# Gate and value products of a SwiGLU block: three float32r passes of split operands in place of seven float32 products

## The chip, the core and the metric

The kernel runs on one core of a Trainium2 chip. The metric is device microseconds (us) of one execution. Five engines work beside each other, each through its own instructions in order: PE (TensorE, the matrix products), DVE (VectorE), ACT (ScalarE), POOL (GpSimd) and SP (SyncE, which issues DMA transfers here). The products accumulate in PSUM, which has eight banks of 128 x 512 float32; all else lies in SBUF.

## The reference

A Mamba-2 scan over 4 batches, 8 heads and 768 positions (head dimension 32, state 16) feeds a SwiGLU block with RMS norm over 3072 tokens, width 256 and hidden width 1536. The weights come in float64.

```python
for c in range(nc):                       # chunks of 32
    CB = einsum('bhin,bhjn->bhij', Cc, Bc)
    y_intra = einsum('bhij,bhjd->bhid', CB * L, xc)       # L: causal decays
    y_inter = einsum('bhin,bhnd->bhid', Cc, state) * decay_to_i
    state = decay_full * state + sum_j(Bx * decay_from_j)
x = y.transpose(0, 2, 1, 3).reshape(3072, 256)
xn = x / sqrt(mean(x * x) + 1e-6) * rms_g
g = xn @ w_gate                           # 3072 x 256 @ 256 x 1536
val = xn @ w_val
return (g * sigmoid(g) * val) @ w_out     # 3072 x 1536 @ 1536 x 256
```

## The kernel before

The tokens go in six blocks of 512. While the gate, value and output products of one block run, the scan of the next block runs between them (transposes `turn`, products `g` and `y`, decays `L`), then its norm (`sq`, `ms`, `rs`, `rb`, `xn`). The normed block `xns[blk]` holds two halves of the width (128 partitions each) by 512 tokens.

**Order.** A string `order` lists about 1550 steps `block:name.numbers`; each step issues a few instructions, and so every engine's queue follows that string. Nothing is moved afterwards. SP's queue gets the transfers in the same order: weights (`fetch`, L160), inputs (`bc`, L121; `x`, L128), decays of later blocks (`spread`, L461), outputs.

**Weights.** Twenty pieces of float64 weights are fetched as pairs of 32-bit words and made into float32 by ACT (`pow`, L182 to L185: the power of two) and DVE (`man`, L192 and L195: the mantissa; `wt`, L201: their product, written to `wgv` or `wo`). All of it lies in block 0.

**Gate and value products.** Block 0 computes columns 0 to 767 (f = 0 to 5, 128 columns each) by plain float32 products (L827, and L837 before the norm is known). Everything else, three pairs of f in block 0 and six pairs in each of blocks 1 to 5, uses Winograd's form of a 2 x 2 block product: seven products instead of eight (`P`, L911) for a pair of f, gate and value side by side in a bank. Each is two float32 matmuls of 128 x 256, and the compiler makes two instructions of one float32 matmul. The form needs sums of weights (`cw`, L881, four DVE instructions for each j), sums of the normed block (`tx`, L888), copies of the running sum out of PSUM (`take`, L917, ACT) and additions (`C`, L923, DVE); then SiLU (`silu`, L932, ACT) and its product with the value (`hid`, L936, DVE). Two banks are tagged gate, two val.

**Output products.** Block 0 uses plain products (`o`, L943); blocks 1 to 5 use the same seven-product form (`O`, L1001) with sums `two` of `w_out` and sums `s`, `s2`, `s3`, `s4` of the hidden tile.

Of the kernel before, what the change touches and what calls it, by code (L numbers as in the profile page):

```python
# [9 lines left out]
FP32 = mybir.dt.float32  # L10
I32 = mybir.dt.int32
I16 = mybir.dt.int16
U32 = mybir.dt.uint32
BF16 = mybir.dt.bfloat16
# [6 lines left out]
def kernel(  # L21
# [108 lines left out]

    wgv = const.tile([P, 2, 2, DF], FP32, name="wgv")
    wg, wv = wgv[:, 0], wgv[:, 1]
# [10 lines left out]
    wdst = {"g": wg, "v": wv, "o": wo}  # L143
# [5 lines left out]
    def fetch(*ks):  # L149
        for k in ks:  # L150
            n, c, w = pieces[k]
            if n == "o":
                src, dst, shape = wsrc[n][:, c:c + w], wo[:, c:c + w], (w, DM)
            else:
                src, dst = wsrc[n][:, :, 2 * c:2 * (c + w)], wdst[n][:, :, c:c + w]
                shape = (2, w)
# [41 lines left out]
    def weight(k):  # L198
        words16, (lo, hi), dst, shape = fetched[k]
        e, f = parts.pop((k, "e")), parts.pop((k, "f"))  # L200
        nc.vector.scalar_tensor_tensor(out=dst, in0=f, scalar=2.0 ** -20, in1=e,  # L201
                                       op0=ALU.mult, op1=ALU.mult)

    a_sb = ffn.tile([BH, S], FP32, tag="ob", name="a_sb", bufs=1)
    warm = const.tile([P, 256], BF16, name="warm")
    gcol = const.tile([P, 2], FP32, name="gcol")
    ident = const.tile([P, P], FP32, name="ident")
    ones = const.tile([P, P], FP32, name="ones")
    upto = const.tile([P, P], FP32, name="upto")
    never = const.tile([P, P], FP32, name="never")  # L210
    after = const.tile([P, P], FP32, name="after")
    chunk_ones = const.tile([P, 2, P], FP32, name="chunk_ones")
# [7 lines left out]
    ident16 = const.tile([P, P], BF16, name="ident16")  # L220
    never16 = const.tile([P, HC], BF16, name="never16")
    whole16 = const.tile([P, P], BF16, name="whole16")
# [11 lines left out]
    la4 = [const.tile([P, 4, 4, NH], FP32, name="la4%d" % k) for k in range(2)]  # L234
# [124 lines left out]
    def three_parts(k):  # L359
        r_ps = ps.pop(("r", k))  # L360
        first = nrm.tile([P, 2, P], BF16, tag="first", name="first", bufs=1)
# [4 lines left out]
        second = nrm.tile([P, 2, P], BF16, tag="second", name="second", bufs=1)  # L366
        nc.vector.tensor_copy(out=second, in_=rest)
        rows[k] = row = const.tile([P, 2, P], BF16, name="row%d" % k)
# [44 lines left out]
    def pair_tile(g):  # L413
        p = g // 2
        if p not in Ls and p < 4:
            Ls[p] = ssd.tile([P, 2, NH, P if p < 2 else HC], FP32, tag="L", name="L", bufs=2)
        elif p not in Ls:
            Ls["of", p // 2] = L = ssd.tile([P, 4, NH, HC], FP32, tag="L", name="L", bufs=2)
            for k in range(2):
                Ls[p - p % 2 + k] = L[:, 2 * k:2 * k + 2]  # L420
# [213 lines left out]
    def states(p):  # L634
        A_ps = ps.pop(("A", p))
        b, c0, chunks = chunks_of(p)
        new = ssd.tile([P, 2, 2, 2, D], FP32, tag="A", name="A")
# [161 lines left out]
    def norm_apply(blk):  # L799
        r = ps["r", blk]  # L800
        xns[blk] = nrm.tile([P, 2, TB], FP32, tag="xn", name="xn", bufs=1)
        if blk:
            for t in range(2):
# [3 lines left out]
        else:  # L807
            nc.vector.tensor_tensor(out=xns[0], in0=yts[0],
                                    in1=r.unsqueeze(1).to_broadcast([P, 2, TB]), op=ALU.mult)

# [29 lines left out]

    def of_block_0(f):
        return hidden_tile(0, f // 2)[:, f % 2].rearrange("p k m -> p (k m)")

    def normed(f):
        gv = ps.pop(("gv", f))
        us[f] = ffn.tile([P, TB], FP32, tag="u", name="u", bufs=2)
# [3 lines left out]
    def silu_of(f):  # L850
        if f not in us:
            us[f] = ffn.tile([P, TB], FP32, tag="u", name="u", bufs=2)
# [16 lines left out]
    Sw, Tx = {}, {}  # L869

    def combine_w(j):
        if j < NF // 4:
            s = raw.tile([P, 2, 4, P], FP32, tag="wr", name="sw", bufs=6)
        else:
            s = const.tile([P, 2, 4, P], FP32, name="sw%d" % j)
        Sw[j] = s
        f1, f2 = slice(2 * j * P, (2 * j + 1) * P), slice((2 * j + 1) * P, (2 * j + 2) * P)
        a11, a12, a21, a22 = wgv[:, :, 0, f1], wgv[:, :, 1, f1], wgv[:, :, 0, f2], wgv[:, :, 1, f2]
        for k, in0, in1, op in ((0, a21, a22, ALU.add), (1, s[:, :, 0], a11, ALU.subtract),
                                (2, a11, a21, ALU.subtract), (3, a12, s[:, :, 1], ALU.subtract)):  # L880
            nc.vector.tensor_tensor(out=s[:, :, k], in0=in0, in1=in1, op=op)  # L881

    def combine_x(blk):
        Tx[blk] = t = nrm.tile([P, 4, 256], FP32, tag="tx", name="tx", bufs=1)
        xn = xns[blk]
        b11, b12, b21, b22 = xn[:, 0, 0:256], xn[:, 0, 256:512], xn[:, 1, 0:256], xn[:, 1, 256:512]
        for k, in0, in1 in ((0, b12, b11), (1, b22, t[:, 0]), (2, b22, b12), (3, b21, t[:, 1])):
            nc.vector.tensor_tensor(out=t[:, k], in0=in0, in1=in1, op=ALU.subtract)  # L888

    half = [slice(0, 256), slice(256, 512)]  # L890
    Xs, Zs, cs, vs = {}, {}, {}, {}

    def product_gv(blk, k, j):
        if k < 4:
            rhs = xns[blk][:, min(k - 1, 1), half[k // 3]]
        else:
            rhs = Tx[blk][:, {4: 3, 5: 0, 6: 1, 7: 2}[k]]
        if k == 1:
            Xs[j] = later[0].tile([P, 512], FP32, tag="gate", name="gate", bufs=2)
        elif k == 2:  # L900
            Zs[j] = later[1].tile([P, 512], FP32, tag="val", name="val", bufs=2)
# [490 lines left out]
```

## Time and profile before

| what | value |
|---|---|
| time, median of 3 runs | 403.92 us (403.78 to 404.91) |
| profiled execution, span from its first to its last instruction | 402.1 us |
| around the span, against the median of the runs | 1.8 us |
| PE busy | 394.8 us in 3881 matmul instructions |
| DVE busy | 297.9 us |
| ACT busy | 224.5 us |
| DMA, moved in all | 26.99 MB |

The profile gives no separate time for the profiled execution beyond its span, so the runs' median is set beside it. A matmul's printed duration includes its way through the array, so instructions overlap: 924 instructions of L911 print 381 ns each, but stand 216 ns apart. Spacing is therefore read from the chain of work that ended last and from the timeline, where start times stand. "Releaser" is the work that an engine was waiting for. DVE's printed durations overlap by some 0.08 us too; the distance between two starts is what one costs.

### The profile page before, as it was taken

How to read it: one execution, taken by the hardware profiler on the slowest of the kernel's cores; microseconds unless marked ns; L12 is line 12 of the kernel's file. 1: busy time of each engine (PE TensorE's matmuls, PEld its weight loads, DVE VectorE, ACT ScalarE, POOL GpSimd, SP SyncE). 2: the span in 40 equal slices, each digit the busy share in tenths (PEclk: the TensorE clock that was granted, in tenths of full speed). 3: DMA queues.
4: the chain of work that ended last, by engine and by line, in shares of the span. 5: the costliest groups of instructions: out<-in, count | busy, mean ns of one | idle time of the engine just before them, and what ended most of it. 6: DMA issues, size and time to landing. Idle time of an engine off the chain costs nothing.

```text
span 402.1 us, 9591 instructions
## 1 busy us (share of the span) xinstructions
PE 394.8 (98%) x3881; PEld 338.9 (84%) x3881; DVE 297.9 (74%) x686; ACT 224.5 (56%) x456; POOL 37.6 (9%) x57
## 2 busy tenths in 40 slices
PE   8989999999999999999999999999999999999997
PEld 5656477888888899888899988899988899988996
DVE  6999999999477997567689467887555767366871
ACT  3989887894684362753572653482645551445410
POOL 2210010001300021200102300021200010000000
PEclk9999999999999999999999999999999999999999
DMA  9989997129012306301223700202000001100001
GB/s 110 189 248 277 178 183 236 38 42 96 2 39 67 68 22 118 79 0 17 68 74 80 104 2 0 44 30 71 27 2 2 2 9 54 52 0 2 0 2 52
DMA packets 92595, 26.99 MB, mean 67 GB/s; under 512 B 77288, under 2 KB 86376, under 8 KB 92552
## 3 DMA queue, kind: packets, MB, share of 16 engines
q1 hardware_dynamic: 88392, 26.13, 30.1%
q10 hardware_dynamic: 4160, 0.26, 0.8%
q8 instruction: 30, 0.49, 0.5%
q14 instruction: 13, 0.11, 0.1%
HBM read 22.64 MB, written 3.74 MB: 66 GB/s over the span
## 4 chain that ended last, share of the span: by engine, by line
PE 91%; SPq 3%; DMA 2%; DVE 1%; ACT 1%; issue 0%
PE gate L911 28%; PE o L1001 24%; PE val L911 21%; PE o L943 5%; PE gate L827 4%; PE y L699 3%; PE gate L837 2%; PE g L562 2%; SPq L121 1%; DMA wr<-in_moe_w_val_dram 1%; PE tp L505 1%; SPq L128 1%; DMA br<-in_B_dram 1%; PE y L627 1%; SPq L160 1%; PE ms L777 0%
## 5 line engine op out<-in xcount | busy, mean ns | idle before, releaser
L923 DVE TENSOR_TENSOR c<-val,p 128x512 f32<-128x512 f32 x99 | 67.5, 688 | 33.8 <-PE val L911 29.6
L917 ACT COPY p<-gate 128x512 f32<-128x512 f32 x99 | 57.4, 581 | 53.2 <-PE gate L911 50.4
L911 PE MATMUL gate<-tx,sw 128*128 128x256 f32 x264 | 65.8, 381 | 0.0
L932 ACT ACTIVATE c<-c 128x256 f32<-128x256 f32 x99 | 39.5, 416 | 44.5 <-DVE c L923 44.5
L911 PEld LDWEIGHTS gate<-tx,sw 128*128 128x128 f32 x264 | 49.5, 190 | 7.1 <-issue 0.3
L936 DVE TENSOR_TENSOR h<-c 128x256 f32<-128x256 f32 x99 | 41.1, 426 | 18.2 <-ACT c L932 18.2
L911 PE MATMUL val<-xn,sw 128*128 128x256 f32 x132 | 33.6, 382 | 0.5 <-DVE c L923 0.5
L911 PE MATMUL val<-tx,sw 128*128 128x256 f32 x132 | 33.6, 383 | 0.1
L911 PE MATMUL val<-xn,wgv 128*128 128x256 f32 x132 | 33.7, 382 | 0.0
L911 PE MATMUL gate<-xn,wgv 128*128 128x256 f32 x132 | 33.4, 380 | 0.0
L911 PE MATMUL gate<-tx,wgv 128*128 128x256 f32 x132 | 33.0, 381 | 0.0
L475 POOL TENSOR_SCALAR_AFFINE_SELECT L<-L 64x512 f32<-64x512 f32 x32 | 23.7, 740 | 87.0 <-ACT L L473 85.8
L1001 PE MATMUL o<-wo,h 128*128 128x128 f32 x240 | 29.9, 276 | 0.0
L1001 PEld LDWEIGHTS o<-wo,h 128*128 128x128 f32 x240 | 28.5, 192 | 0.5 <-issue 0.2
L1001 PE MATMUL o<-two,h 128*128 128x128 f32 x240 | 28.9, 276 | 0.0
L1001 PE MATMUL o<-two,s 128*128 128x128 f32 x240 | 28.9, 276 | 0.0
L911 PEld LDWEIGHTS val<-xn,sw 128*128 128x128 f32 x132 | 24.8, 190 | 4.2 <-DVE c L923 0.9
L1001 PEld LDWEIGHTS o<-two,s 128*128 128x128 f32 x240 | 28.0, 192 | 0.4 <-issue 0.2
L911 PEld LDWEIGHTS val<-tx,sw 128*128 128x128 f32 x132 | 24.7, 190 | 3.9 <-DVE c L923 0.5
L1001 PEld LDWEIGHTS o<-two,h 128*128 128x128 f32 x240 | 27.8, 192 | 0.2 <-DVE s L967 0.2
L911 PEld LDWEIGHTS gate<-tx,wgv 128*128 128x128 f32 x132 | 24.8, 190 | 3.5 <-ACT c L932 0.2
L911 PEld LDWEIGHTS val<-xn,wgv 128*128 128x128 f32 x132 | 24.8, 190 | 3.5 <-issue 0.2
(188 smaller groups left out, 614.1 us busy)
## 6 DMA issues: line engine op xcount, KB each, us to landing
L<-rowd SPq DMA_DIRECT2D x32, 128.0 KB, 3.0
xr<-in_x_dram SPq DMA_DIRECT2D x24, 128.0 KB, 4.7
wr<-in_moe_w_out_dram SPq DMA_DIRECT2D x6, 512.0 KB, 7.0
wr<-in_moe_w_val_dram SPq DMA_DIRECT2D x5, 512.0 KB, 6.4
wr<-in_moe_w_gate_dram SPq DMA_DIRECT2D x5, 512.0 KB
out_dram<-ob SPq DMA_DIRECT2D x9, 256.0 KB, 2.2
br<-in_B_dram SPq DMA_DIRECT2D x22, 64.0 KB
cr<-in_C_dram SPq DMA_DIRECT2D x22, 64.0 KB, 2.4
```

The source lines that it names most:

```text
L475: nc.gpsimd.affine_select(out=L[r], in_=L[r], pattern=[[0, NH], [1, HC]], compare_op=ALU.is_ge, fill=0.0, base=0, channel_multiplier=-1)
L562: nc.tensor.matmul(out=g[u, P * i:P * i + P].rearrange("p (t m) -> p t m", t=2), lhsT=T[r, i, 0, u], rhs=T[r, i, 1:3, u], start=(first and ...
L699: nc.tensor.matmul(out=y[2 * k + u][rows, (2 * n + i) * HC:(2 * n + i + 1) * HC], start=(k, u, rows.start) not in opened, stop=True, skip_ ...
L827: nc.tensor.matmul(out=gv[:, k], lhsT=w[:, t, fs], rhs=xns[0][:, t], start=(t == 0), stop=(t == 1))
L837: nc.tensor.matmul(out=gv[:, k, tk], lhsT=w[:, t, fs], rhs=yts[0][:, t, tk], start=(s == 0 and t == 0), stop=(t == 1), skip_group_check=True)
L911: nc.tensor.matmul(out=dst[:, half[w]], lhsT=lhsT, rhs=rhs, start=(k in (1, 2, 5) and w == 0), stop=True, skip_group_check=True)
L917: nc.scalar.copy(out=t, in_=Xs[j])
L923: nc.vector.tensor_tensor(out=t, in0=Zs[j], in1=a, op=ALU.add)
L932: nc.scalar.activation(out=u, in_=src[:, half[0]], func=AF.Silu)
L936: nc.vector.tensor_tensor(out=hidden_tile(blk, j)[:, c // 10 - 1, c % 10 - 1], in0=u, in1=src[:, half[1]], op=ALU.mult)
L943: nc.tensor.matmul(out=o, lhsT=hs_[blk, f // 2][:, f % 2, k // 2, (k % 2) * P:(k % 2 + 1) * P], rhs=wo[:, f], start=opens, stop=(f == NF - ...
L1001: nc.tensor.matmul(out=o[t] if apart else o[:, t * P:(t + 1) * P], lhsT=lhsT[:, t], rhs=rhs, start=(k in (1, 2, 4, 5) and j == 0 and (apar ...
```

## The change

Three float32r matmuls of 512 tokens replace the seven products. Each operand is split into a leading part (its low 12 bits masked off by an integer AND) and a rest: `xm`, then `xs = xm * ONE - x`, `xl = xm / BETA - xs` and a copy `xh` of the leading part; for the weights `top`, `s` and `m` in the same way (`sw`, two calls for each j where `cw` was one, with twice as many columns in each instruction). A bank first gets the cross product of the two differences (`D`: two matmuls, over the two halves of the width), ACT scales it where it lies (`W`, PSUM to the same PSUM), and four more matmuls add to it (`G`). SiLU and the hidden product read the bank directly, 512 columns at a time, scaled by `ONE`. `take`, `C`, `cw` and `tx` go.

`wgv` becomes float32r. `wt` writes float32 pieces elsewhere, and DMAs on SP's queue copy eight of them into `wgv` (`keep`: four of 128 KB, four of 256 KB) and later twelve leading parts of 256 KB (`kt`). Constants of the start share the buffers of the hidden tiles; the decays `L` of blocks 1 to 5 have one buffer in place of two; `xn` is computed in place of `yt`. The order string is new throughout: `fetch.5` comes before the second `x`, inputs such as `x.4` come later, `two.0`, `man.19` and `wt.19` move behind the first products of block 1, and so do four of block 0's twelve output products (`o.7`, `o.9`, `o.10`, `o.11`; before, `o.11` alone).

```diff
+    BETA = 4096.0
+    ONE = 1.0 + 1.0 / BETA
+    wgv = const.tile([P, 2, 2, DF], FP32R, name="wgv")
+    wgvf = wgv.bitcast(FP32)
+    wg, wv = wgvf[:, 0], wgvf[:, 1]
+    wearly = const.tile([P, 2, 2, 256], FP32, tag="sw3", name="wearly")
...
         e, f = parts.pop((k, "e")), parts.pop((k, "f"))
-        nc.vector.scalar_tensor_tensor(out=dst, in0=f, scalar=2.0 ** -20, in1=e,
-                                       op0=ALU.mult, op1=ALU.mult)
+        nc.vector.scalar_tensor_tensor(out=f if dst is None else dst, in0=f, scalar=2.0 ** -20,
+                                       in1=e, op0=ALU.mult, op1=ALU.mult)
+        if dst is None:
+            parts[k, "w"] = f
+
+    def keep(k):
+        n, c, w = pieces[k]
+        src = wearly[:, "gv".index(n), :, c:c + w] if c < 256 else parts.pop((k, "w"))
+        nc.sync.dma_start(out=wgv[:, "gv".index(n), :, c:c + w].bitcast(FP32), in_=src)
...
-        if p not in Ls and p < 4:
-            Ls[p] = ssd.tile([P, 2, NH, P if p < 2 else HC], FP32, tag="L", name="L", bufs=2)
+        if p not in Ls and p < 2:
+            Ls[p] = ssd.tile([P, 2, NH, P], FP32, tag="L%d" % p, name="L", bufs=1)
         elif p not in Ls:
-            Ls["of", p // 2] = L = ssd.tile([P, 4, NH, HC], FP32, tag="L", name="L", bufs=2)
+            Ls["of", p // 2] = L = ssd.tile([P, 4, NH, HC], FP32, tag="L0", name="L", bufs=1)
...
         r = ps["r", blk]
-        xns[blk] = nrm.tile([P, 2, TB], FP32, tag="xn", name="xn", bufs=1)
         if blk:
+            xns[blk] = yts[blk]
...
+    def leading(out, of):
+        nc.vector.tensor_scalar(out=out.bitcast(I32), in0=of.bitcast(I32), scalar1=-4096,
+                                scalar2=None, op0=ALU.bitwise_and)
+
+    def leading_x(blk, t):
+        xm[blk, t] = nrm.tile([P, TB], FP32, tag="sq2" if t else "sq", name="xm", bufs=1)
+        leading(xm[blk, t], xns[blk][:, t])
+
+    def rounded_x(blk, t, engine):
+        if blk not in xh:
+            xh[blk] = nrm.tile([P, 2, TB], FP32R, tag="xn", name="xh", bufs=1)
+        engine(out=xh[blk][:, t], in_=xm[blk, t])
+
+    def differences_x(blk, t):
+        if blk not in xs:
+            xs[blk] = nrm.tile([P, 2, TB], FP32R, tag="xs", name="xs", bufs=1)
+        nc.vector.scalar_tensor_tensor(out=xs[blk][:, t], in0=xm[blk, t], scalar=ONE,
+                                       in1=xns[blk][:, t], op0=ALU.mult, op1=ALU.subtract)
+
+    def trailing_x(blk, t):
+        if blk not in xl:
+            xl[blk] = nrm.tile([P, 2, TB], FP32R, tag="xl", name="xl", bufs=1)
+        nc.vector.scalar_tensor_tensor(out=xl[blk][:, t], in0=xm[blk, t], scalar=1.0 / BETA,
+                                       in1=xs[blk][:, t].bitcast(FP32), op0=ALU.mult,
+                                       op1=ALU.subtract)
...
-    def combine_w(j):
-        if j < NF // 4:
...
-            nc.vector.tensor_tensor(out=s[:, :, k], in0=in0, in1=in1, op=op)
...
-                lhsT = Sw[j][:, w, {5: 0, 6: 1, 7: 2, 3: 3}[k]]
-            nc.tensor.matmul(out=dst[:, half[w]], lhsT=lhsT, rhs=rhs,
-                             start=(k in (1, 2, 5) and w == 0), stop=True, skip_group_check=True)
...
-    def taken_gv(blk, k, j):
-        vs[k, j] = t = cvt.tile([P, 512], FP32, tag="e", name="p", bufs=4)
-        nc.scalar.copy(out=t, in_=Xs[j])
-    def total_gv(blk, c, j):
-        a = vs.pop(({11: 1, 12: 6, 22: 7}[c], j))
-        cs[c, j] = t = raw.tile([P, 512], FP32, tag="ws", name="c", bufs=4)
-        nc.vector.tensor_tensor(out=t, in0=Zs[j], in1=a, op=ALU.add)
...
+        w = parts.pop((2 + 2 * j + k, "w")) if j >= 3 else wgvf[:, k, :, 256 * j:256 * j + 256]
+        s, m = Sw[j][:, k], Mw[j][k]
+        tops[j, k] = top = cvt.tile([P, 2, 256], FP32, tag="e", name="top", bufs=4)
+        leading(top, w)
+        nc.vector.scalar_tensor_tensor(out=s, in0=top, scalar=ONE, in1=w, op0=ALU.mult,
+                                       op1=ALU.subtract)
+        nc.vector.scalar_tensor_tensor(out=m, in0=s.bitcast(FP32), scalar=-BETA, in1=top,
+                                       op0=ALU.mult, op1=ALU.add)
+
+    tops = {}
+
+    def keep_top(j, k):
+        nc.sync.dma_start(out=wgvf[:, k, :, 256 * j:256 * j + 256], in_=tops.pop((j, k)))
+
+    GV = {}
+
+    def cross_gv(blk, f, k):
+        GV[f, k] = g = later[k].tile([P, TB], FP32, tag="val" if k else "gate", name="gv", bufs=2)
+        for t in range(2):
+            nc.tensor.matmul(out=g, lhsT=Sw[f // 2][:, k, t, (f % 2) * P:(f % 2 + 1) * P],
+                             rhs=xs[blk][:, t], start=(t == 0), stop=True, skip_group_check=True)
+
+    def weigh_gv(blk, f, k):
+        nc.scalar.activation(out=GV[f, k], in_=GV[f, k], func=AF.Copy,
+                             scale=-BETA * BETA / (BETA + 1.0))
+
+    def main_gv(blk, f, k):
+        for t in range(2):
+            for lhsT, rhs in ((wgv[:, k, t, f * P:(f + 1) * P], xh[blk][:, t]),
+                              (Mw[f // 2][k][:, t, (f % 2) * P:(f % 2 + 1) * P], xl[blk][:, t])):
+                nc.tensor.matmul(out=GV[f, k], lhsT=lhsT, rhs=rhs, start=False, stop=True,
+                                 skip_group_check=True)
+
+    def silu_gv(blk, f):
+        us[f] = cvt.tile([P, TB], FP32, tag="e", name="u", bufs=4)
+        nc.scalar.activation(out=us[f], in_=GV.pop((f, 0)), func=AF.Silu, scale=ONE)
+
+    def hide_gv(blk, f):
+        nc.vector.scalar_tensor_tensor(out=hidden_of(blk, f), in0=GV.pop((f, 1)), scalar=ONE,
+                                       in1=us.pop(f), op0=ALU.mult, op1=ALU.mult)
```

The new order has 1451 steps. In block 0 it has `sw` for j = 3, 4, 5, 1 and 0 (its first half) before the differences `xs.1` of block 1; the rest of `sw` follows them.

## The prediction

> **What bounds the kernel now.** First the page: who is busy, and who owns the chain that ended last.
>
> ```profile
> span 402.1 us, 9591 instructions
> ...
> PE 394.8 (98%) x3881; PEld 338.9 (84%) x3881; DVE 297.9 (74%) x686; ACT 224.5 (56%) x456; POOL 37.6 (9%) x57
> ...
> DVE  6999999999477997567689467887555767366871
> ...
> PEclk9999999999999999999999999999999999999999
> ...
> PE 91%; SPq 3%; DMA 2%; DVE 1%; ACT 1%; issue 0%
> PE gate L911 28%; PE o L1001 24%; PE val L911 21%; PE o L943 5%; PE gate L827 4%; PE y L699 3%; PE gate L837 2%; PE g L562 2%; SPq L121 1%; DMA wr<-in_moe_w_val_dram 1%; PE tp L505 1%; SPq L128 1%; DMA br<-in_B_dram 1%; PE y L627 1%; SPq L160 1%; PE ms L777 0%
> L923 DVE TENSOR_TENSOR c<-val,p 128x512 f32<-128x512 f32 x99 | 67.5, 688 | 33.8 <-PE val L911 29.6
> L917 ACT COPY p<-gate 128x512 f32<-128x512 f32 x99 | 57.4, 581 | 53.2 <-PE gate L911 50.4
> ```
>
> PE is the bound, at full clock, and L911 is 49% of the chain. The digits of DVE are also 9 in the first quarter, so the work by stages comes next (columns: stretch; its length; busy us and instructions of PE, PEld, DVE, ACT, POOL; clock; DMA share; GB/s).
>
> ```profile
> 25.00:45.00 20.00, 20.00 (x191) 12.32 (x192) 19.28 (x40) 19.02 (x31) 1.02 (x1) 1.00 0.92 268
> 80.00:100.00 20.00, 20.00 (x97) 17.64 (x96) 18.91 (x40) 14.63 (x23) 1.73 (x2) 1.00 0.56 69
> 160.00:220.00 60.00, 60.00 (x644) 53.87 (x643) 43.65 (x98) 31.24 (x65) 7.41 (x9) 1.00 0.22 53
> ```
>
> Two regimes: block 0 (to about 98 us) has PE and DVE both full; blocks 1 to 5 have a full PE and a DVE at 73%. Then the chain, for the spacing of matmuls (start, length, what):
>
> ```profile
> 29.52 1.73 PE gate L837 x8
> 31.24 0.43 PE e L426 x2
> ...
> 36.35 3.43 PE gate L827 x8
> ...
> 97.75 0.86 PE gate L911 x4
> ```
>
> An instruction of 128x256 float32 costs 0.216 us (1.73 for 8), one of 128x512 float32 0.43, and the bf16 one of 128x512 (L426) 0.215. With two instructions in a float32 matmul, float32 costs four times bf16. And DVE's own line, where starts are the price:
>
> ```profile
> 49.47 0.42 DVE L881 TENSOR_TENSOR sw<-wgv 128x256 f32<-128x256 f32 x1
> ...
> 50.94 0.42 DVE L488 TENSOR_TENSOR Bd<-br,d_sb 128x256 f32<-128x256 f32 x1
> 51.27 0.42 DVE L192 TENSOR_SCALAR m<-wr 128x512 int32<-128x512 int32 x1
> 51.73 0.69 DVE L195 SCALAR_TENSOR_TENSOR m<-wr,m 128x512 f32<-128x512 uint32 x1
> 52.34 0.68 DVE L860 TENSOR_TENSOR h<-u,gate 128x512 f32<-128x512 f32 x1
> ...
> 94.05 1.41 DVE L804 SCALAR_TENSOR_TENSOR xn<-yt,gcol,r 128x512 f32<-128x512 f32 x2
> ```
>
> From 19 to 102 us DVE waits about 1 us in all: in block 0, each added DVE operation moves what follows it.
>
> **PE's work.** Before: 33 pairs of f (3 in block 0, 30 later) x 7 products x 4 instructions = 924, x 0.216 = 199.6 us. After: each pair has 2 f x 2 (gate, value) x 6 = 24 matmuls of 128x512; 792 in all. No row shows float32r. Its ends: 0.215 (bf16 of that shape) and 0.43 (one float32 instruction of that shape; two of them would be 0.86). I take 0.216, since the split leaves only leading bits in an operand and so needs one narrow product per matmul, as bf16 does. That is 171.1 us: 28.5 less, of which 2.6 in block 0 and 25.9 in blocks 1 to 5. Weight loads, one per pass, stay hidden: L911's 190 ns load fits in 216 ns today.
>
> The Trainium skill (TensorE: Matmul & The Clock Gate, Part 3, The mechanism) says that a weight load overlaps a running matmul only when it targets another row group, which speaks against many full-array passes. By it a pass would be 216 + 190 = 406 ns and the change would cost 122 us more than the old products. The trace disagrees: four loads and four passes of L911 on all 128 rows take 0.86 us.
>
> Switches between float32r and float32: L426 ran right after float32 at 0.43 for two, so 0 extra; the far end is 0.2 (L837's x8 takes 1.93 instead of 1.73 after the small tiles), times some 88 switches in blocks 1 to 5, 18 us. I take 0, the nearer kind: data type, not tile.
>
> **DVE in block 0.** The first product of block 1 (97.75) came after `xn.1` (95.4). In the new order it needs `xs.1`, which stands behind more of DVE's work. Starts give: `cw` 1.47 (49.47 to 50.94), C 0.60, `hid` 0.34, `tx` 1.46, `two` 1.47, a mantissa plus product (`man`, `wt`) 1.67. Gone or moved later: 4 x 1.47 + 9 x 0.60 + 11 x 0.34 + 1.46 + 1.47 + 1.67 = 19.6. For the new: AND 0.46 (L192 to L195), scalar_tensor_tensor 0.61 to 0.66 (L195, L804), 0.11 more when it needs the one just before. So `sw` = 0.46 + 0.72 + 0.61 = 1.79. Nine before `xs.1`: 16.1; `hidg` 5 x 0.66 = 3.3; block 0's split 2 x (0.46 + 0.65 + 0.65) = 3.5; block 1's `xm`, `xs` 2.2. Sum 25.1, net +5.5: `xs.1` is done at 100.9.
>
> PE has less to do until then: 72.7 us between 25 and 97.75, less 1.5 idle, less 2.6, less three output products of 1.73 that now come later = 63.4. So it idles 100.9 - 25 - 63.4 = 12.5 us there, against 1.5: 11.0 more (the 2.6 and the moved products are counted in the work, so nothing is counted twice). From there to the first `G` DVE needs another `hidg`, `sw` and two `xl` (3.8) while PE has four `D` and one output product (3.5): 0.3 more. Block 0's loss 11.3. Its low end is 0, if DVE's 4 idle us before 20 and other order make it up; its high end 17, if copying adds to it.
>
> **Copies and queues.** `keep` moves 1.5 MB while the DMA engines are 92% busy at 268 GB/s: 5.6 us of transfer, and SP gets 20 more issues of some 0.5 us in block 0, each waiting for DVE with the fetches behind it. Cost 0: no DVE work waited for weights (their only waiter was ACT, 1.7 us), and the new order puts `x.4` out of that stretch. Without this cover 6 us. The Trainium skill (DMA: Bandwidth & Descriptors, Where 436 GB/s comes from) puts SBUF-to-SBUF copies at 435 GB/s, which would make an estimate of 3.4 us; the sum does not use it.
>
> **The new wait.** `D` - `W` - `G`: `G` waits for ACT. From the last `D`: 0.29 until the result is out (L426 prints 508 ns at 215 spacing), 0.06 of handoffs, 0.58 for `W` (L917; writing to PSUM from ACT is in no row, ends 0.42 to 1.02 by L932 and the slowest ACT row): 0.93. Behind `G` stands all of PE's queue. Summing PE's steps between each `D` and its `G` in blocks 1 to 5 (0.43 a `D`, 0.86 a `G`, 0.45 an `O`): median 2.15, but 22 of 120 have under 0.94 and 39 under 1.6. ACT's load hardly moves: -18 `take` - 24 `silu` + 24 `W` + 12 wider `silu` + 2 `xh` = +2.0 us a block, 33 of 55. I take 3 us of stalls; ends 0 and 23 (39 x 0.58, one ACT operation ahead of each).
>
> **At nothing.** DVE in blocks 1 to 5 falls by 9 us a block. The hidden product waits for SiLU over 512 columns; its two val banks cover it. One `L` buffer in place of two: `spread` of a block must now follow `y` of the one before; half a block lies between, more than the 3 us of its transfers. If that cover went, about 3 us a block.
>
> **Sum.** 402.1 - 28.5 + 11.3 + 3 = 387.9, plus the 1.8 us between the profiled span and the median of the runs: 389.7.
>
> **Rivals.**
> - *Block 0 loses nothing* (DVE catches up, as 25.9 of 28.5 lies elsewhere): 402.1 - 28.5 + 3 + 1.8 = 378.4. For it: idle DVE before 20. Against it: +5.5 on a full engine. 0.16.
> - *`W` becomes the bound*: ACT is busy half the time when a `D` ends, so 39 x 0.29 = 11.3 in place of 3: 398.0. For it: the 33 us of 55 that ACT is busy. Against: ACT may start a `W` well ahead, median cover 2.15. 0.16.
> - *Slower: a float32r pass costs more than a bf16 pass.* The forecast's gain of 14.2 us is gone at 216 + 14.2 / 792 = 234 ns a pass. At 0.43 the time is 389.7 + 792 x 0.215 = 560. For it: no row shows the type. Against: the split's narrow operands. 0.11.
> - *It levels out* (pass near 234 ns, or stalls of 17): within 0.3%, 1.2 us. 0.02.
>
> **How the numbers follow.** The forecast gets 0.55: 389.7. The range 377 to 401 takes in the first two rivals and the unknown ends between; it leaves out the slow pass and stalls beyond 14 us. 0.3% is about what a measurement here can tell from no change. Faster 0.55 + 0.16 + 0.16 = 0.87, same 0.02, slower 0.11.
>
> **What would show it.** Right: matmuls of 128x512 float32r spaced 0.216 in the chain; PE gaps of some 12 us before block 1's first products, ended by DVE; blocks 1 to 5 some 5 us shorter each (60 to 55). Wrong: a spacing over 0.234; PE waiting for ACT's `W` over 3 us in all; PE without gaps in block 0.

## The result

The changed kernel takes 434.39 us (median; 433.31 to 436.91) where the kernel before takes 404.01 (403.78 to 404.91): a ratio of 1.0755, 95% interval 1.0715 to 1.0796. The forecast, 389.7 in a range of 377 to 401, has the wrong sign. The profiled execution has a span of 431.6 us against 402.1.

### The profile page after: what moved, and what is told of

Its sections match the earlier page's. It is cut to its first block, busy times and chain, and to the rows that moved or that the text cites. A ratio compares the mean times of both kernels' runs of the same rounds, so it can differ in the third digit from the quotient of the medians.

```text
span 431.6 us, 9229 instructions
## 1 busy us (share of the span) xinstructions
PE 400.3 (93%) x3749; PEld 318.5 (74%) x3749; DVE 255.9 (59%) x545; ACT 256.9 (60%) x450; POOL 38.4 (9%) x57
## 4 chain that ended last, share of the span: by engine, by line
PE 72%; DVE 10%; ACT 7%; DMA 3%; issue 3%; SPq 3%; ACTq 0%; DVEq 0%
PE gv L963 24%; PE o L1033 18%; PE gv L952 13%; PE o L975 3%; PE y L711 3%; PE gate L868 2%; SPq L122 1%; PE g L567 1%; PE g L574 1%; DVE m L200 1%; DMA wr<-in_moe_w_val_dram 1%; DVE S L663 1%; DMA roots<-r 1%; DVE L L479 1%; DMA cr<-in_C_dram 1%
## 5 line engine op out<-in xcount | busy, mean ns | idle before, releaser
L963 PE MATMUL gv<-xh,wgv 128*128 128x512 f32 x264 | 109.1, 413 | 3.4 <-DMA wgv<-top 2.0
L963 PE MATMUL gv<-xl,mw 128*128 128x512 f32 x264 | 104.5, 396 | 0.0
L956 ACT ACTIVATE gv<-gv 128x512 f32<-128x512 f32 x132 | 73.7, 587 | 40.6 <-PE gv L952 40.0
L971 DVE SCALAR_TENSOR_TENSOR h<-gv,u 128x512 f32<-128x512 f32 x66 | 45.2, 689 | 81.3 <-PE gv L963 72.4
L952 PE MATMUL gv<-xs,sw 128*128 128x512 f32 x264 | 79.0, 411 | 2.8 <-DVE h L971 2.5
L968 ACT ACTIVATE u<-gv 128x512 f32<-128x512 f32 x66 | 39.5, 603 | 45.8 <-PE gv L963 43.9
L963 PEld LDWEIGHTS gv<-xh,wgv 128*128 128x128 f32 x264 | 50.1, 190 | 20.0 <-ACT gv L956 9.4
L952 PEld LDWEIGHTS gv<-xs,sw 128*128 128x128 f32 x264 | 45.9, 189 | 15.5 <-DVE h L971 4.0
L963 PEld LDWEIGHTS gv<-xl,mw 128*128 128x128 f32 x264 | 50.2, 190 | 9.4 <-DVE xl L848 0.2
L1033 PEld LDWEIGHTS o<-wo,h 128*128 128x128 f32 x240 | 31.2, 191 | 1.6 <-ACT u L968 0.4
L975 PE MATMUL o<-wo,h 128*128 128x256 f32 x96 | 22.2, 379 | 0.0
```

What stands on the lines that cost most here:

```text
L952: nc.tensor.matmul(out=g, lhsT=Sw[f // 2][:, k, t, (f % 2) * P:(f % 2 + 1) * P], rhs=xs[blk][:, t], start=(t == 0), stop=True, skip_group_ ...
L956: nc.scalar.activation(out=GV[f, k], in_=GV[f, k], func=AF.Copy, scale=-BETA * BETA / (BETA + 1.0))
L963: nc.tensor.matmul(out=GV[f, k], lhsT=lhsT, rhs=rhs, start=False, stop=True, skip_group_check=True)
L968: nc.scalar.activation(out=us[f], in_=GV.pop((f, 0)), func=AF.Silu, scale=ONE)
L971: nc.vector.scalar_tensor_tensor(out=hidden_of(blk, f), in0=GV.pop((f, 1)), scalar=ONE, in1=us.pop(f), op0=ALU.mult, op1=ALU.mult)
L975: nc.tensor.matmul(out=o, lhsT=hs_[blk, f // 2][:, f % 2, k // 2, (k % 2) * P:(k % 2 + 1) * P], rhs=wo[:, f], start=opens, stop=(f == NF - ...
```

## The profile after

The page of the changed kernel, head and chain:

```profile
span 431.6 us, 9229 instructions
...
PE 400.3 (93%) x3749; PEld 318.5 (74%) x3749; DVE 255.9 (59%) x545; ACT 256.9 (60%) x450; POOL 38.4 (9%) x57
...
DVE  5555869799899547864355863446823434713551
...
PEclk9657895899999999999999999999999999999999
...
PE 72%; DVE 10%; ACT 7%; DMA 3%; issue 3%; SPq 3%; ACTq 0%; DVEq 0%
```

PE has 132 instructions fewer and is busy for 5.5 us more; DVE, which had 9s in the first quarter, begins with 5s; and the line of the granted clock, all 9s before, has holes up to 80 us. Only 72% of the chain is PE's, where 91% was. The same windows by stage (columns as in the prediction):

```profile
0.00:25.00 25.00, 18.56 (x126) 10.51 (x127) 13.60 (x51) 13.83 (x27) 5.15 (x17) 0.76 0.71 146
25.00:45.00 20.00, 17.57 (x174) 10.83 (x174) 12.68 (x28) 12.03 (x20) 1.46 (x2) 0.67 0.46 117
45.00:62.00 17.00, 15.08 (x85) 9.31 (x83) 11.91 (x22) 13.45 (x21) 0.00 (x0) 0.94 0.71 203
62.00:80.00 18.00, 9.42 (x67) 4.54 (x68) 15.94 (x31) 10.91 (x16) 0.00 (x0) 0.62 0.97 169
80.00:100.00 20.00, 20.00 (x368) 14.68 (x366) 18.75 (x48) 15.45 (x37) 2.24 (x2) 1.00 0.56 169
...
160.00:220.00 60.00, 58.75 (x630) 49.51 (x629) 32.41 (x73) 35.34 (x68) 7.74 (x10) 1.00 0.30 56
```

Between 25 and 45 us DVE did 19.28 us of work before and does 12.68 now, and the clock stands at 0.67. Three marks on PE's line cut the time into parts that can be compared in every kernel below: the first gate product (the first `gate<-yt` in the timeline), block 1's first product (before, the first `gate<-xn` behind `xn.1`, 97.75 in the chain; after, the twenty-fifth `gv<-xs`), and the end. The forecast's row is worked out from its sum: 387.9 less 101.

| | first gate product | block 1's first product | from there to the end |
|---|---|---|---|
| before | 25.5 | 97.8 | 304.3 |
| forecast | (no loss named) | 101 | 286.9 |
| after | 38.0 | 123.1 | 308.5 |

So the 29.5 us lost against before are 12.5 until the first gate product, 12.8 in the rest of block 0, and 4.2 behind it; the 44 us by which the forecast was off are 22.1 in block 0 and 21.6 behind it. These are two different errors.

**The start.** The timelines of ACT and PE, changed kernel (start, length, what; in brackets the idle time before and what ended it):

```profile
9.93 0.38 ACTq L122 DMA_DIRECT2D br<-in_B_dram  x1
11.16 0.46 ACTq L122 DMA_DIRECT2D cr<-in_C_dram  x1
11.66 0.52 ACT L415 ACTIVATE early<-full_ps 128x416 f32<-128x416 f32 x1 [6.12 <-DMA cr<-in_C_dram]
```

```profile
7.10 0.68 PE L369 MATMUL r_ps<-mids,lead 128*128 128x256 f32 x2
12.23 0.94 PE L391 MATMUL d_ps<-la,lead 128*128 128x192 f32 x4 [4.45 <-ACT early L415]
...
18.16 2.08 PE L567 MATMUL g<-T 32*128 32x256 f32 x8
```

`bc.1` stands later in the new order, behind `d`. ACT issues two of its loads, and each issue waited for the end of an earlier transfer (`fetch.5`, `fetch.0` and `x` had been put ahead of it): the trace has the two transfers landed at 9.90 and 11.14, and the issues at 9.93 and 11.16. `cx` (L415) stands behind these issues in ACT's queue and came 6.1 us late; `d`'s bank needs `cx`, so PE stood for 4.45 us. From 13.0 to 36.9 us the trace then shows PE's clock at half: the 32 matmuls of L567 take 7.5 us there by their starts (4.2 in e12 below, at full clock).

**The rest of block 0.** What DVE waited for, from the first gate product to block 1's first product, in the kernel before (25.5 to 97.8) and after (38.0 to 123.1):

```profile
DVE A L641 <- PE y L627: 0.8, 2, 0.4
DVE wo L201 <- ACT e L185: 0.6, 2, 0.3
DVE u L848 <- PE gate L837: 0.3, 1, 0.3
DVE c L923 <- PE val L911: 0.2, 1, 0.2
```

```profile
DVE r_sb L1114 <- ACT e_sb L1121: 2.8, 1, 2.8
DVE wearly L206 <- ACT e L190: 1.6, 1, 1.6
DVE h L904 <- ACT u L897: 1.5, 1, 1.5
DVE yt L770 <- ACT sq L752: 1.5, 1, 1.5
DVE wo L206 <- ACT e L190: 1.2, 1, 1.2
DVE m L206 <- ACT e L190: 1.1, 2, 0.8
...
```

DVE's own work in the two stretches is 3 us apart: it is busy for 69.0 us of the 72.3 before and for 72.1 us of the 85.1 after. Its waits were 1.9 us and are 11.7, so of the 12.8 us lost there some 10 are waits and 3 are work.

**Blocks 1 to 5.** What the weight loads waited for there (in the first and the last line 23 and 16 waits, most of them a few tenths or less), and below it PE:

```profile
PEld gv L963 <- ACT gv L956: 6.5, 23, 1.8
...
PEld gv L952 <- DVE h L971: 3.7, 4, 1.9
PEld gv L952 <- ACT u L968: 3.5, 16, 0.4
```

```profile
PE gv L952 <- DVE h L971: 2.5, 2, 1.5
...
PE gv L963 <- ACT gv L956: 1.3, 1, 1.3
```

Passes that follow each other stand 231 ns apart (median; quarters 229 and 236), not 216. The 720 passes take 179.8 us by the distance of their starts, where 840 instructions of L911 took 183.5.

## The experiments

The times in one table (e5, which measures passes alone, is not in it); the intervals are 95%. The three columns at the right are from the profiled execution of each. (Stretches of half clock in blocks 1 to 5, none to 17 us in all, differ from execution to execution: the granted clock of e10's four is 0.945 to 0.960. So the last column and the medians of the later versions move by a few us without an edit there, and the intervals of e12, e13 and e14 overlap: their times are not told apart.)

| run | edit | median | ratio to before | first gate | block 1 | to the end |
|---|---|---|---|---|---|---|
| e1 | copies issued by POOL | 447.4 | 1.1075 (1.0941 to 1.1210) | 38.9 | 127.9 | 320.0 |
| e2 | `bc.1` early | 424.3 | 1.0504 (1.0443 to 1.0565) | 29.2 | 115.8 | 307.8 |
| e3 | both | 442.3 | 1.0951 (1.0884 to 1.1018) | 29.0 | 120.6 | 319.0 |
| e4 | no `W` | 434.6 | 1.0758 (1.0707 to 1.0810) | 34.8 | 121.7 | 310.4 |
| e6 | first order of before | 425.5 | 1.0533 (1.0409 to 1.0657) | 25.7 | 111.2 | 310.8 |
| e7 | e2 with matmuls in the gaps | 421.6 | 1.0436 (1.0342 to 1.0530) | 31.2 | 112.5 | 308.4 |
| e8 | e6, three waits mended | 423.1 | 1.0448 (1.0400 to 1.0495) | 24.9 | 111.7 | 309.4 |
| e9 | e8, table loads together | 421.3 | 1.0400 (1.0372 to 1.0429) | 25.3 | 112.5 | 308.2 |
| e10 | e2, late copies | 431.3 | 1.0637 (1.0575 to 1.0699) | 29.4 | 116.1 | 315.2 |
| e11 | e9, late copies | 415.1 | 1.0280 (1.0256 to 1.0305) | 26.6 | 105.9 | 307.4 |
| e12 | e11, two waits mended | 410.1 | 1.0152 (1.0117 to 1.0187) | 25.3 | 102.9 | 305.5 |
| e13 | e12, `Td.3` early | 411.0 | 1.0146 (1.0112 to 1.0179) | 25.3 | 100.3 | 306.3 |
| e14 | e13, `sw.1` late | 412.0 | 1.0183 (1.0155 to 1.0211) | 24.9 | 99.2 | 313.4 |

### e1, e2, e3: SP's queue or the gap at the start

```diff
-        nc.sync.dma_start(out=wgv[:, "gv".index(n), :, c:c + w].bitcast(FP32), in_=src)
+        nc.gpsimd.dma_start(out=wgv[:, "gv".index(n), :, c:c + w].bitcast(FP32), in_=src)
...
-        nc.sync.dma_start(out=wgvf[:, k, :, 256 * j:256 * j + 256], in_=tops.pop((j, k)))
+        nc.gpsimd.dma_start(out=wgvf[:, k, :, 256 * j:256 * j + 256], in_=tops.pop((j, k)))
```

> The changed kernel with its twenty SBUF-to-SBUF copies (keep, kt) issued from POOL's queue instead of SP's. Theory S (SP's queue is blocked by copies that wait for DVE, 19.2 us in all, and the weight fetches behind them come late): SP's waits for wearly are gone, the first gate product (45.5 us in the changed kernel) starts at 33 to 38, time about 424. Theory C (the halved TensorE clock after a PE gap at 7.4 us sets the start): the gap and the clock of 0.5 from 13 to 37 us stay, the first gate product stays beyond 42, time over 430.

```diff
-        0:fetch.5 0:whole 0:mask.0.0/0 0:eps 0:upto 0:mid 0:upto2 0:bc.0 0:tmask
+        0:fetch.5 0:whole 0:mask.0.0/0 0:eps 0:upto 0:mid 0:upto2 0:bc.0 0:bc.1 0:tmask
...
-        0:c*2 0:after2 0:mids 0:r.0 0:d 0:bc.1 0:turn.0.1
+        0:c*2 0:after2 0:mids 0:r.0 0:d 0:turn.0.1
```

> The changed kernel with one step of the order moved: bc.1 right behind bc.0, ahead of fetch.0. Theory C: ACT no longer waits 6.1 us for a DMA before chunk decays, PE's gap of 4.8 us at 7.4 goes, the clock stays at 1.0 in the first 40 us, the first gate product starts at 34 to 38 and the time is about 425. Theory S: the clock is mended, but the weights still come late; the first gate product stays beyond 41, time over 429.

e3 has both edits.

> Both edits together. If S and C are separate causes their gains add: first gate product near 28 to 30, time about 414 to 417. If they are one and the same delay, no better than the better of the two, about 424.

(The expectations of e1 and e2 count from the second group of gate products, which starts at 45.3 in the changed kernel, 45.9 in e1 and 37.6 in e2; the table counts from the first.) The copies on POOL's queue took SP's waits for `wearly` away and made the kernel 13 us slower. POOL's own work (`L`'s mask, the sums of squares) now stands in one queue with copies that wait for DVE and PE (15.2, 12.4, 10.7 and 10.2 us in all in e1's longest rows); that this is the reason is argued from these waits. Theory S falls: with `bc.1` mended, the first gate product came at 29.2 with the copies on SP and at 29.0 with them on POOL. One step moved forward (e2) brought 8.8 us until the first gate product, and 10.1 in all. e3's 442.3 misses both of its times: the two edits do not add. `cx` now follows its operand:

```profile
5.40 0.43 ACT L326 ACTIVATE lead<-early 128x128 f32<-128x128 f32 x2
7.12 0.52 ACT L415 ACTIVATE early<-full_ps 128x416 f32<-128x416 f32 x1 [1.28 <-PE full_ps L410]
```

### e4: the wait of `G` for `W`

```diff
-        "W": lambda f, k: weigh_gv(0, f, k),     # and "W": weigh_gv in blocks 1 to 5
+        (all W steps left out of the order)
```

The cross products stay unscaled, so this kernel leaves out a part of the product.

> The changed kernel without the W steps (the scaling of the cross product in its bank is left out, so that part of the values is wrong); G follows D at once on PE. Theory W (the wait of G for ACT sets blocks 1 to 5): the stretch from block 1's first product to the end, 313 us, shortens by 8 to 14 us. Theory P (the float32r pass itself costs 0.230 instead of 0.216 and the rest is the end of other chains): it shortens by under 4 us, and the median distance of two float32r passes stays near 230 ns.

The passes of blocks 1 to 5 took 178.5 us in place of 179.8, and 1.4 us of these went to a longer stretch of half clock: `W` costs 1 to 3 us there. The whole stretch to the end did not shorten (310.4 against 308.5, with 13.7 us at half clock in place of 3.4). Theory W falls as an explanation; as a term (3 us in the forecast) it fits.

### e5: the pass by itself

A kernel that holds nothing but groups of 48 passes, and twelve chains of two passes, an ACT operation in the bank, four passes:

```diff
+    for k in range(48):
+        nc.tensor.matmul(out=dst(k), lhsT=lhs(wr, k), rhs=rhs(wr, k), **first(k))
```

> Only the disputed passes, one group after another, nothing else on the chip's engines; the kernel's own computation is left out whole. Groups of 48 matmuls with 128x128 weights that change at every pass, 512 columns: bf16, float32r; then float32r with weights of 64 columns, float32r with one and the same weights, float32r and bf16 with 256 columns, float32 with 256 and with 512 columns; last, twelve times two passes, an operation of ACT in place in the bank, four passes. Theory P (the pass itself costs more than a bf16 pass): float32r with 512 columns is spaced 229 to 233 ns here too, bf16 214 to 217. Rival contention (the 15 ns come from DVE, ACT and the DMAs beside it): float32r 214 to 217 here. If the weight load sets it, weights of 64 columns or unchanged weights bring it down to 216; if the stream of columns does, those stay at 231 and the pass of 256 columns takes about half, 115. The wait of D, W, G alone: 0.29 + 0.06 + 0.58 = 0.93 us between the start of the last D and the first G by the prediction's working.

The timeline of PE (L63 bf16; L65, L67, L69 float32r, L67 with 64 columns of weights and L69 with one and the same weights; L71 float32r and L73 bf16 with 256 columns; L75 float32 with 256 columns):

```profile
6.90 12.03 PE L63 MATMUL bank<-w 128*128 128x512 bf16 x48 [6.90 <-DVE w L44]
18.58 11.26 PE L65 MATMUL bank<-wr 128*128 128x512 f32 x48
29.68 11.20 PE L67 MATMUL bank<-wr 128*64 128x512 f32 x48
40.72 11.04 PE L69 MATMUL bank<-wr 128*128 128x512 f32 x48
51.60 5.91 PE L71 MATMUL bank<-wr 128*128 128x256 f32 x48
57.36 5.41 PE L73 MATMUL bank<-w 128*128 128x256 bf16 x48
62.61 10.53 PE L75 MATMUL bank<-wf 128*128 128x256 f32 x48
```

Starts divided by 48: float32r 231, with 64 columns of weights 230, with one weight 227; medians 227, 229, 227. The bf16 pass is 216 (median; its first eight ran at half clock), float32 of 256 columns 216. With 256 columns float32r takes 120 and bf16 109. So a float32r pass costs 11 ns more than a bf16 pass, at 512 and at 256 columns alike, with a short or an unchanged weight as well: the surcharge belongs to the pass, neither to its columns nor to the weight load. Contention falls as a rival, and so do weight load and columns as its source; theory P's band, 229 to 233, was a little high. The kernel adds 4 ns to these 227. Alternating one float32r pass of 512 with two float32 instructions of 128 columns took 454 ns a round (316, 108 and 30 by starts) against 227 + 216: at most 6 ns a switch, so the forecast's zero for switches stands. The chain alone took 1.05 us from the start of the last `D` to the first `G` (0.42 until ACT starts, 0.58, 0.05), the forecast's 0.93.

### e6: the order of before until the banks change

The first 240 steps in the order of before, with `sw`, `xm`, `xs`, `xl`, `xh` in the places of `cw` and `tx`, and each `keep` a few steps behind its `wt`:

```diff
-        0:warm 0:zeros 0:a 0:never 0:idle.7 0:ones 0:ident 0:after 0:whole16 0:kinks 2:exps
+        0:warm 0:a 0:set 0:bc.0 0:ident 0:bc.1 0:ones 0:x.0 0:zeros 0:mean 0:head 0:upto 0:x.1
...
-        0:keep.2 0:yt.1 0:bc.2 0:mask.2/2 0:parts.1 0:sums.3 0:man.6 0:wt.6
+        0:keep.5 0:parts.1 0:man.6 0:mask.3/1 0:sums.3 0:pow.2 0:wt.2 0:rowe.0 0:dT.2
```

> The changed kernel with the order of before for the first 240 steps (to the change of banks), in which the split of x and w takes the places of the copies that it replaces, the keep copies come a few steps after their weights, and the early table loads are left out. Theory O (the new order of block 0's start costs, through PE gaps and the half clock behind them): first gate product at 25 to 28 us, no half clock before 60, block 1's first product at 105 to 112, the time 408 to 420. Rival A (the arithmetic does it: 20 copies and the split on a full DVE, in whatever order): block 1's first product stays at 115 or later, the time 423 or more. Blocks 1 to 5 keep their 308 to 313 us by both.

The start is that of before again (first gate product 25.7, no half clock until 35), so all 12.5 us lost there were the order's. The rest of block 0 did not follow: 85.5 us from the first gate product, as after (85.1) and in e2 (86.6). Block 1's first product, 111.2, is in theory O's band; the time, 425.5, misses its 408 to 420 and lies in the rival's. The waits have other names now; DVE's and PE's longest until block 1:

```profile
DVE m L197 <- DMA wgv<-m: 7.4, 2, 6.4
...
PE tp L517 <- ACT sq L759: 5.4, 1, 5.4
...
PE gate L878 <- DVE yt L770: 4.2, 1, 4.2
```

The first is a copy (`keep.5`) that holds a buffer that DVE wants.

### e7: what half clock costs by itself

```diff
-        0:early.0.0/0      ...  0:gg.2/1
+        0:early.0.0*18/0   ...  0:hot*28 0:gg.2*40/1      # matmuls of bf16 zeros ahead of the bank's use
```

> The order of bc.1 early, with matmuls of bf16 zeros put into three gaps of PE: 18 ahead of the first gate products, 28 and 40 ahead of the products of the third pair's g. They compute nothing that is used. Theory C (the half clock behind a gap costs time of its own): half-clock stretches behind 31 and 57 us gone, block 1's first product 3 to 8 us earlier than the 115.8 of bc.1 early, time 416 to 421. Rival D (DVE is the bound from 50 to 116 us and PE has slack at either clock): the clock is full there and the time stays within 2 us of 424.3.

The fillers took the places of the two longest gaps (28 and 40 matmuls at 51.8 and 54.8):

```profile
51.77 3.22 PE L88 MATMUL hot<-lead 128*128 128x256 bf16 x28
54.82 4.53 PE L88 MATMUL g<-lead 128*128 128x256 bf16 x40
59.28 0.69 PE L575 MATMUL g<-T 32*64 32x128 f32 x32
```

Half clock behind 31 us and behind 57 us (20.5 us of it in e2) shrank to 3.4 us; block 1's first product came 3.3 us earlier and the span was 2.7 us shorter. Both theories hold in part: half clock cost some 3 us there, a fifth of its length; that PE mostly waited for DVE in those stretches is the likely reason, not shown by itself.

### e8, e9: waits mended, table loads together

```diff
-        0:L.1.1 0:y.0/1 0:sq.0 0:fetch.12 0:row.1 0:pow.3 0:rowout.1 ... 0:wt.5 ... 0:early.0.0/0 0:keep.5
+        0:L.1.1 0:y.0/1 0:sq.0 0:fetch.12 0:wt.5 0:keep.5 0:row.1 0:pow.3 0:rowout.1 ... 0:early.0.0/0
...
-        0:y.2/2 0:yt.2 0:xh.0.0 0:xh.0.1 0:xl.0.0 0:sq.2      (0:xl.0.1 after 0:turn.3)
+        0:xl.0.0 0:xl.0.1 0:pow.10 0:y.2/2 0:yt.2 0:xh.0.0 0:xh.0.1 0:sq.2
```

> The kernel with the first order of before, with three waits that its trace showed taken away by order alone: the copy keep.5 goes right behind its weight (DVE waited 6.4 us for it), both xl go ahead of the squares of the third pair (PE waited 5.8 us there), the copies kt.5.1, kt.3.0 and kt.3.1 go right behind their splits (PE waited 2.4 us). Theory O (waits that the order makes, not DVE's work, cost block 0; DVE's work there is 63 us in every version): block 1's first product at 98 to 105 us in place of 111.2, the time 411 to 418. Rival A (DVE is full there): it stays at 108 or later, the time 420 or more. By both, the 300 us behind it stay at 308 to 311, so that the time stays above the 403.6 of before.

```diff
-        0:rs.1 ... 0:exps        0:ex.10 0:sw.0.1 0:ex.11 ... 0:ex.9       1:exps ... 1:silu.9
+        0:exps 0:rs.1            0:sw.0.1 ... 0:ex.10 0:ex.11 0:ex.9       1:silu.9 ... 1:exps
```

> The kernel of the mended order, and in blocks 1 to 5 the steps of ACT that need one function table stand together (five steps moved, one preload moved, three added): some 10 loads of 1.28 us fewer. Theory T (the table loads, 36 against the 21 of before, delay W and SiLU and so PE in blocks 1 to 5): block 1's first product to the end takes 303 to 306 us in place of 308 to 311. Rival (PE has cover for ACT there; what is lost is the price of the passes and the turn of the banks): less than 1.5 us of difference.

Theories O and T both missed. In e8 the waits of 6.4, 5.8 and 2.4 us went or shrank, others came in their places, and block 1's first product stayed at 111.7. (The 63 us that the expectation gives for DVE's work are too low: it is busy for 72.2 us of e6's stretch, 69.0 before.) The longest in block 0:

```profile
PE y L639 <- DVE Bd L500: 5.0, 1, 5.0
PE gate L878 <- DMA wgv<-wearly: 3.5, 2, 2.2
PE g L574 <- DVE S L661: 3.4, 1, 3.4
```

```profile
DVE m L197 <- DMA wgv<-m: 4.6, 2, 3.0
DVE Bd L500 <- DMA br<-in_B_dram: 3.3, 1, 3.3
DVE u L892 <- PE gate L878: 2.4, 1, 2.4
```

Two of these are copies (L878 waits for `wearly`'s, DVE for a buffer that one holds). e9 had 21 table loads in place of 36, as many as before, and won 1.2 us behind block 1's first product, as its rival had it: theory T falls.

### e10, e11: no product waits for a copy

The products of the first six f read float32 weights from the tiles that DVE writes; the eight copies follow later:

```diff
-    wearly = const.tile([P, 2, 2, 256], FP32, tag="sw3", name="wearly")
+    wearly = [const.tile([P, 2, 2, 256], FP32, tag=tag, name="wearly") for tag in ("sw3", "mw4", "sw5")]
...
-                nc.tensor.matmul(out=gv[:, k], lhsT=w[:, t, fs], rhs=xns[0][:, t],
+                nc.tensor.matmul(out=gv[:, k], lhsT=w[:, t], rhs=xns[0][:, t],
...
-        0:keep.2 0:yt.1      (each keep behind its wt)
+        0:early.1.1 0:keep.0 0:keep.1 0:keep.2 0:keep.3 ... 0:gate.2/0 0:keep.5 0:keep.4 ... 0:gate.3/2 0:keep.6 0:keep.7
```

> The order of bc.1 early, but the products of the first six f read their float32 weights from the tiles that DVE writes; the eight copies into the float32r tile are issued later (behind early.1.1, gate.2 and gate.3), so that no product of block 0's start waits for one and none holds a buffer of DVE. Theory K (the copies cost block 0's middle, as a wait in front of the early products, as holders of DVE's buffers, as blockers of SP's queue): from the first gate product to block 1's first product 77 to 82 us in place of 86.6, the time 414 to 420. Rival A' (the order's other waits, of DVE for ACT and of PE for DVE, remain or move): 84 us or more, the time 422 or more.

> The same late copies in the kernel of the mended order with the table loads together. Theory K: DVE's waits for copies (5.9 us) and PE's (4.0 us) are gone, from the first gate product to block 1's first product 77 to 82 us in place of 87.2, the time 410 to 416. Rival A': 84 us or more, the time 418 or more. In either case the 308 us behind block 1's first product stay within 1.5 us.

The same edit does nothing in the order of the change (e10: block 1's first product at 116.1 against 115.8; the profiled execution is the slowest of its four, 433.0 us, and has 17 us of half clock in blocks 1 to 5) and 6.6 us in the order of before (e11: 105.9 against 112.5, time 415.1 in the expected 410 to 416). Copies cost about what the forecast set down for them without cover, 6 us, but only where nothing else is late at the same place.

### e12, e13, e14: DVE's line to `xs.1`

```diff
-        0:hid.2 0:pow.8 ... 0:kt.3.1 0:bc.3        0:sw.4.0 ... 0:Tt.3.0 0:sw.4.1 0:S.3
+        0:hid.2 0:bc.3 0:pow.8 ... 0:kt.3.1        0:yt.2 0:S.3 ... 0:sw.4.0 ... 0:Tt.3.0 0:sw.4.1
```

> The kernel of late copies in the mended order, with the two longest PE waits left in its block 0 mended by order: bc.3 goes ahead of the first split copies in SP's queue (PE waited 4.9 us for its data through DVE), S.3 goes ahead of sw.4.0 on DVE (PE waited 3.2 us). Theory O/K (block 0's loss is a sum of such waits, each gone when its order is mended): block 1's first product at 97 to 101 us in place of 105.9, about the 97.8 of before; the time 406 to 411. Rival (the waits move to the next step, as they did in the mended order with early copies): 104 us or more, the time 413 or more. Neither gets below the 403.8 of before, since the blocks behind take 307 us against 304.3.

```diff
-        0:Tt.3.0 0:sw.4.1 0:x.4 0:G.6.0 0:Tt.3.1 0:D.7.1 0:Td.3
+        0:Tt.3.0 0:Td.3 0:sw.4.1 0:x.4 0:G.6.0 0:Tt.3.1 0:D.7.1
```

> The version with two waits mended, and Td.3 ahead of sw.4.1 on DVE (PE waited 4.1 us for it). If DVE's line to xs.1 sets block 1's first product (102.9, right behind xs.1), PE's 4.1 us come back only as far as DVE waited for PE behind them (2.6 us): first product at 100 to 101, the time 407 to 408. If PE's line sets it, 98.8 and 406.

```diff
-        0:wt.16 0:sw.1.0 ... 0:kt.1.0 ... 0:sw.1.1 ... 0:kt.1.1 ... 1:D.0.0 ... 0:kt.0.1
+        0:wt.16 ... 1:D.0.0 ... 0:kt.0.1 0:sw.1.0 0:kt.1.0 0:sw.1.1 0:kt.1.1
```

> The same, and the two splits sw.1 with their copies (2 x 1.79 us of DVE) behind block 1's first products instead of ahead of xs.1. DVE's line: first product at 96.5 to 97.5, the blocks behind unchanged at 305.5 to 307 unless 1:D.2 now waits for sw.1; the time 403.5 to 406, no better than the 403.8 of before: DVE's line in block 0 and the price of a pass then leave nothing of the exchange. A time under 402.5 would say that the exchange itself gains and that only the order lost it.

The windows of e12:

```profile
0.00:25.00 25.00, 21.76 (x251) 13.36 (x252) 20.89 (x68) 16.48 (x34) 5.76 (x18) 1.00 1.00 194
25.00:45.00 20.00, 20.00 (x192) 12.12 (x192) 19.59 (x39) 19.31 (x32) 0.73 (x1) 1.00 0.90 270
45.00:62.00 17.00, 13.32 (x161) 7.27 (x159) 15.88 (x35) 12.34 (x25) 1.31 (x1) 0.90 0.85 130
```

The first 45 us are those of before (25 to 45: PE 20.00, DVE 19.28, clock 1.00 there), and the time, 410.1, is in the expected 406 to 411; block 1's first product, 102.9, lies between the two bands. In e13 DVE's last steps ahead of block 1 read (the column after the start is the length)

```profile
98.08 0.69 DVE L481 TENSOR_TENSOR L<-L,tok 128x512 f32<-128x512 f32 x1
98.69 1.29 DVE L844 SCALAR_TENSOR_TENSOR xs<-xm,yt 128x512 fp32r<-128x512 f32 x2
```

and PE's first product stands at 100.3: `xs.1` is done at 100.0, where the forecast had 100.9. With most of the order's waits gone, DVE's line sets block 0's end nearly as it was worked out. Block 1's first product is in its 100 to 101; e13's best time, 408.3 us, lies just above its 407 to 408 and the median, 411.0, well above. e14 shortened DVE's line by less than reckoned (99.2, not 97), and then `G` of block 1 waited 2.3 us for `xl`, which a moved split now precedes; with 3.4 us at half clock behind that wait, its 412.0 misses the expected 403.5 to 406. Nothing that was run beats the kernel before.

## Why the prediction was wrong

**The order was never priced.** The step that failed is the one on DVE in block 0: "From 19 to 102 us DVE waits about 1 us in all: in block 0, each added DVE operation moves what follows it." That is a reading of the order of before, and the sum carried it into an order that is new in every step. (Even there its waits are 1.9 us, not 1, and all its idle time is 3.5.) The count of work was near: until `xn.1` is done DVE is busy for 88.0 us before, until `xs.1` is done for 93.9 after and 92.6 in e13, so 5.9 and 4.6 us more, where the forecast had 5.5. The premise of a full DVE was what failed: until the same points it stands idle for 7.4 us before, 29.5 after, and again 7.4 in e13. The start, where the forecast saw 4 us of idle DVE as a possible gain and named no loss, cost 12.5 us, 8.8 of them through one moved step (e2). e13, with the same arithmetic and the copies late, recovers 22.8 us until block 1's first product (123.1 to 100.3); e2's step alone brought 7.3. The forecast had looked at `x.4` among the moved transfers, not at `bc.1`, whose two issues on ACT's queue stood in front of `cx`.

**The clock was not in the forecast at all.** Before, it is 1.00 until the end. After, the trace shows half clock for 44 us, 41 of them in block 0. Its price is less than its length: e7 puts 3 us on 17 us less of it. The Trainium skill (TensorE: Matmul & The Clock Gate, Part 1: The HAM clock gate) says that PE falls to half its clock after an idle window of about 3.4 us and is back after as much work. The lengths agree (3.4, 6.8, 10.2, 13.7, 23.9 us, multiples of 3.41); the trigger was shorter here (in e2 PE was idle for 1.87 us, 2.24 from start to start at 10.8, and half clock began within that gap and lasted 10.2 us), and 23.9 us passed before it was back although PE was busy for 23.0 of them by its printed durations.

**The pass.** The term was mis-sized: "I take 0.216, since the split leaves only leading bits in an operand and so needs one narrow product per matmul, as bf16 does." It is 231 ns in the kernel and 227 alone, 11 ns over bf16 at both widths measured. 792 x 15 = 11.9 us of the 28.5 are gone. The rival's bound, 234 ns, was right, and 231 lies just inside it: by the price of the pass alone the forecast would have been 401.6, and faster. The part on weight loads was right: full-array loads of 190 ns stay hidden at 227 ns, against the sentence that the forecast weighed there (the same section also lets a load run ahead into a background weight buffer, which this fits).

**Behind block 1's first product** 308.5 in place of 286.9. The passes take 179.8 us where the sum had 155.5 and 3 of stalls. By the distance of starts the 24.3 us over 155.5 are 10.8 for the price of 720 passes, 4.2 in seven distances over 345 ns at full clock (two of them 1.7 and 1.9 us), 3.4 in short delays within runs of passes and ahead of small tiles, 1.5 behind small tiles, 1.4 at half clock, and 3.1 behind output products, which is only a shift (the output product in front is shorter by as much, 31 ns for 112). The releasers named are `W`, the hidden product that frees a bank, and SiLU. e4 gives `W` 1 to 3 us, so the 3 us taken for it and its ends of 0 and 23 fit; e9 clears the table loads, and a switch costs at most 6 ns (0.5 us for 88). That the rest, some 6 to 8 us, is the turn of two banks that now hold a pair from `D` to `hid` is argued from those rows, not shown: the kernel has all eight banks in use, and no run has a third bank there.

**Copies.** The forecast's 0, and 6 without cover, came out in both halves (e10: 0; e11: 6.6), but by luck: the 6 us were transfer time at 268 GB/s, and what costs is what waits for a copy, or for the buffer that it reads. The 3 MB of the twelve `kt` were priced as issues alone; PE waited 2.0 us for one of them after.

**Rivals.** None of the four was what happened; the third had the direction of the pass right, and its 234 ns was not reached. Half of the error had no rival: an order that loses time by itself.

**What the exchange is worth.** In e12 and e13 block 0 ends 2.5 to 5 us later and the rest takes 1 to 2 us longer than before, for an exchange that gives PE 16.6 us less work on paper (924 x 0.216 - 792 x 0.231). Block 0 gives its share back on DVE, and blocks 1 to 5 (15.1 us by that count, against 5.2 of moved output products) give theirs back in waits and short delays of PE. Whether an order exists in which more of it stays was not found out.

## What to carry to other kernels

When an order is rewritten, a stall-free profile of the old one says nothing of the new one: list, for every engine, what stands behind each moved step that can wait (a DMA issue on a compute engine's queue above all), and keep "the new order loses time by itself" as a rival with a price. Test that rival first, since it is cheap: the old order with the new arithmetic in its places recovered 9 of 30 us here (e6), and 24 once the copies came late and single waits were mended (e12). And a wait that is taken away is worth what the next one leaves of it: e8 went for three waits of 14.6 us together and gained nothing at block 1's first product, and the edit that did nothing in one order (e10) was worth 6.6 us in another.

## What the hardware showed that was not expected

- A float32r pass costs 11 ns over a bf16 pass at both widths measured (e5): 227 against 216 at 512 columns, 120 against 109 at 256. Weights of 64 columns (229) and unchanged weights (227) do not lower it.
- With 1.87 us of idle PE came 10.2 us at half clock (e2), with 4.45 us came 23.9 (after); all stretches inside the runs are multiples of 3.41 us.
- Moving twenty copies from SP's queue to POOL's cost 13 us (e1), 18 with `bc.1` early (e3 against e2).
- A DMA issue can hold its engine until an earlier transfer ends: ACT's two issues of `bc.1` went out at 9.9 and 11.2 us; with `bc.1` ahead of the other transfers `cx` behind them came 4.5 us earlier.
